# Chunk 0's copies shared by two engines, and ScalarE passes moved ahead of the first join

## The chip, the cores and the metric

The kernel runs on one core of a Trainium2 chip. The metric is the time of one execution on the device in microseconds; of several runs the median is taken. The core's engines are called TensorE (PE, its weight loads PEld), VectorE (DVE), ScalarE (ACT), GpSimd (POOL) and SyncE (SP), as in the profile. Each takes its own instructions strictly in the order in which the program issues them; where one needs what another makes, it waits for it. SP issues most of the DMAs of this kernel, in order too.

## The reference

Two blocks, one behind the other: a linear attention with a delta rule (4 batches, 8 heads, 768 steps, head width 48), and a SwiGLU feed-forward block (3072 tokens, 384 in, 1536 within).

```python
def _attn_ref(q, k, v, beta):
    k_n = k / (np.linalg.norm(k, axis=-1, keepdims=True) + 1e-06)
    state = np.zeros((B, H, D, D), dtype=np.float32)
    for t in range(S):
        kt, vt, bt = (k_n[:, :, t], v[:, :, t], beta[:, :, t, None])
        y[:, :, t] = np.einsum('bhd,bhde->bhe', q[:, :, t], state)
        v_old = np.einsum('bhde,bhd->bhe', state, kt)
        state = state + bt[:, :, :, None] * np.einsum('bhd,bhe->bhde', kt, vt - v_old)

def _moe_ref(x, w_gate, w_val, w_out):
    g = x @ w_gate
    silu = g * (1.0 / (1.0 + np.exp(-g)))
    return (silu * (x @ w_val) @ w_out).astype(np.float32)
```

## The kernel before

**Tiling.** The 768 steps are cut into 12 chunks of 64. Within a chunk the recursion is turned into matrix products: a triangular 64 by 64 matrix per head and batch, made of products of k with itself, must be inverted; with the inverse Z, a chunk is a short row of products. The inverses are made for two chunks at once (a group g). `substitute` (L483) does the forward substitution of blocks of 32 by 32 on DVE, in 31 steps of two operations (L488, L494); a join then makes the lower left block of each 64 by 64 inverse on PE.

**One chunk.** `advance(c)` (L708) is a generator; each `step("advance", advance, c)` runs it to its next yield. Its parts: for c over 0 the products with the old state; then p_u, the inverse times v (L741), copied to uu (L752), and the loads of v of chunk c+2 (`load_v`, L160); then p_y (L760), copied to y with its halves turned (L793, L795); then six transposes p_f (L805), copied to xts[c], shown as x_ffn (L808), which is the input of the feed-forward block for this chunk's 256 tokens. For chunk 0 a fifth part makes the first state (`of_state`, L769, copied by ACT at L783). The name `each` (L750) splits the copies of chunk 0 by bp, the pair of batches.

**Feed-forward.** `gate_val(c, f, fill, within)` (L818) makes p_gate and p_val in 12 matmuls each (L825), sil on ACT (L834) and h on DVE (L840). Between its parts it calls `fill` and `point`, which put other work at these places of each engine's order. `output` (L848) makes the result.

**Weights.** The three weight matrices are brought in as pieces: 0 to 11 are 256 columns wide (w_gate and w_val in turn), 12 to 23 are 512, and from 24 on pieces of w_out. A piece is loaded as 32-bit words into whatever tile is free (`stage`, L222; `place_of` names the place, `freed_by` the piece behind which a place is free again) and then converted. `power_step(n)` (L236) is the part on ACT: two passes, one that writes into the weight tile (L244) and one that writes an array of powers into one of the tiles hp[10] to hp[13] (L250). `convert(ns)` (L252) calls it for its pieces if it has not been done, does three operations for each piece on DVE (L261, L269, L281), calls `power_step` for some pieces ahead (L277 to L279), and then stages the pieces whose places have come free. Pieces 0 to 11 use hp[10] to hp[13] in turn, two to a tile; pieces 12 and 13 use hp[10] and hp[12].

**The order around the change.** Nothing is scheduled by a planner here: the block under `tc.manual_schedule` (L1112) is the order of every engine. After the substitution of group 0 (with ACT's passes of pieces 0 to 3 put into its middle, L1170), it runs: `turned_m(1, "ffn")` (L558), PE transposes that leave the matrix M of group 1 in two banks of PSUM, to be copied to mb; the scaling of v (L374); `turned(1, True, "px")`, q of chunk 1, copied by ACT at L412. Then `late_z` (L572): two DVE transposes, into zt (L574) and d_t (L580). Then `join_late(0, 0, ...)` (L583) for chunk 0, in two parts. Its first part copies half of d_t to d_o (L591, two copies), makes a first product (L598), and scales it into t2 (L600, shown as t). Its second part makes p_j (L608) and copies it into the upper right block of zt (L616, four copies: e, the parity of the head, by two quarters of the partitions). The generator `first_q` holds chunk 0's product of q and k: its second part is the masking on DVE (L437) into p_sb, which p_y reads.

The rest of the order before the first gate is six calls `converts(2)` with the steps of `advance` for chunk 0 and the copies of M between them, at L1182 to L1199. `invert(1)` (L619) begins with POOL's square root n_b of M's diagonal (L633); the rest of it comes much later, through `fill`. `second` is the join of chunk 1; it is run through the list `first`, inside the first `gate_val`, together with chunk 0's state.

The lines of the order that matter:

```python
        for _ in late_z(0, zb):
            pass
        mb = new_mb()
        mbs.append(mb)
        first_join = join_late(0, 0, ("px", "py"))
        next(first_join)
        converts(2)
        next(first_q)
        next(first_join)
        nc.scalar.copy(mb[:, m_1[0][0]], m_1[0][1])
        step("advance", advance, 0)
        converts(2)
```

Of the kernel before, what the change touches and what calls it, by code (L numbers as in the profile page):

```python
# [20 lines left out]
def kernel(  # L21
# [25 lines left out]
    nc = tc.nc  # L47
# [130 lines left out]
    pieces = []  # L178
# [4 lines left out]
    N_HALF = sum(piece[4] < PIECE for piece in pieces)  # L183
# [65 lines left out]
        )  # L249
        nc.scalar.activation(power, words_of[:, :, 0], ACTF.Copy, scale=2.0**-29)  # L250

    def convert(ns):  # L252

        work_of = []
        for n in ns:
            dst, _, t, f0, m = pieces[n]
            power_step(n)
            place = staged.pop(n)[:, 0:m]
            work_of.append((dst[:, t, f0 : f0 + m].bitcast(U32), place, powers.pop(n)))
        for dst, place, _ in work_of:  # L260
            nc.vector.tensor_scalar(  # L261
                out=place,
                in0=dst,
                scalar1=3,
                scalar2=None,
                op0=ALU.logical_shift_left,
            )
        for dst, place, _ in work_of:
            nc.vector.scalar_tensor_tensor(  # L269
                out=dst,  # L270
                in0=dst,
                scalar=0x80000000,
                in1=place,
                op0=ALU.bitwise_and,
                op1=ALU.bitwise_or,
            )
        for n in range(ns[-1] + 1, ns[-1] + 7):  # L277
            if n < min(N_HALF, len(pieces)) or ns[-1] + 3 > n < len(pieces):
                power_step(n)  # L279
        for dst, _, power in work_of:  # L280
            nc.vector.tensor_tensor(out=dst, in0=dst, in1=power, op=ALU.add)  # L281
        for n in ns:
            for later in freed_by.get(n, ()):
                stage(later)
# [27 lines left out]
    def half_of(x):  # L312
        return slice(64 * x, 64 * x + 64)
# [74 lines left out]
    def turned(c, of_q, tag=None):  # L388

        tag = tag or ("py" if of_q else "px")  # L390
        x = qpad[c % QB] if of_q else knp[slot(c)]
        if of_q:
            xt = work.tile([128, NB * NJ * 2 * C], FP32, name="qt", bufs=1)
        else:
            xt = kts[slot(c)]
        if c >= blocks_of[of_q][1]:
            xt_v = xt.rearrange("p (bp b j i) -> p bp j b i", bp=NB, b=2, j=NJ)
            (qt if of_q else kt)[c] = xt_v
            blocks = blocks_of[of_q][2]
            nc.vector.transpose(xt, blocks.rearrange("p bp h d -> p (bp h d)"))  # L400
            if c + 1 < NCH:
                load_blocks(of_q, c + 1)
            return
        xt = xt.rearrange("p (bp j b i) -> p bp j b i", bp=NB, j=NJ, b=2)
        (qt if of_q else kt)[c] = xt
        p_t = banks("p_t", tag)
        for bp in range(NB):
            for j in range(NJ):
                at = slice(128 * j, 128 * j + 128)
                nc.tensor.transpose(p_t[bp][:, at], x[:, bp, 2 * j : 2 * j + 2], ident)  # L410
        for bp in range(NB):
            nc.scalar.copy(xt[:, bp].rearrange("p j b i -> p (j b i)"), p_t[bp])  # L412
        if of_q and c + QB < Q_BLOCKS:
            load_q(c + QB)
# [46 lines left out]
    z1s, mbs = {}, []  # L461
    WAIT = 2

    def new_mb():
        return work.tile([128, R, R], FP32, name="mb", bufs=1)
# [114 lines left out]
        nc.vector.transpose(z_late[g], zb)  # L580
        yield

    def join_late(g, c, tags):  # L583


        zt, a, d_t = ztp[g % ZB], a_sb[g], z_late[g]
        M = HH // 2
        d_o = work.tile([128, M, R], FP32, name="d_o", tag="z1", bufs=1)
        d_v = d_t[:, :, HH * c : HH * c + HH].rearrange("p k (m e) -> p e m k", e=2)
        for s in range(2):  # L590
            nc.scalar.copy(d_o[QUADS[2 * s + 1][0]], d_v[QUADS[2 * s][0], 1])  # L591
        p_j = banks("p_j", tags[0])[0][:, 0 : M * R].rearrange("p (m i) -> p m i", i=R)
        for m in range(M):
            for e in range(2):
                for s in range(2):
                    dst, lo = QUADS[2 * s + e][0], QUADS[2 * s + 1][0]
                    h = 2 * m + e
                    nc.tensor.matmul(p_j[dst, m], a[lo, c, h, 0:R], zt[lo, c, h, R:C])  # L598
        t2 = work.tile([128, M, R], FP32, name="t2", tag="tmp", bufs=1)
        nc.scalar.mul(t2, p_j, -1.0)  # L600
        yield
        p_j = ps_pair("p_j", tags[1]).rearrange("p e (m i) -> p e m i", i=C)
        for of_d in (True, False):
            for m in range(M):
                for e in range(2):
                    for s in range(2):
                        row, hi = QUADS[2 * s + e][0], QUADS[2 * s][0]
                        nc.tensor.matmul(  # L608
                            p_j[hi, e, m, 0:R] if of_d else p_j[hi, e, m, R:C],
                            d_o[row, m] if e else d_t[row, :, HH * c + 2 * m],  # L610
                            ident[row, row] if of_d else t2[row, m],
                        )
        zt_v = zt[:, c].rearrange("p (m e) i -> p e m i", e=2)
        for e in range(2):
            for hi in (QUADS[0][0], QUADS[2][0]):
                nc.scalar.copy(zt_v[hi, e], p_j[hi, e])  # L616
        yield

    def invert(g):  # L619
# [88 lines left out]
    def advance(c):  # L708
# [80 lines left out]
            of_state()  # L789
        p_of_u()  # L790
        y = work.tile([128, NB, NJ, 2, D], FP32, name="y", tag="r", bufs=2)
        for bp in each:
            nc.scalar.copy(y[:, bp, :, 0], p_y[:, 0, bp])  # L793
            for b in range(2):
                nc.scalar.copy(y[half_of(b), bp, :, 1], p_y[half_of(1 - b), 1, bp])  # L795
        yield

        y_f = y.rearrange("p bp j par d -> p bp (j par d)")
# [5 lines left out]
                at = slice(t * 128, (t + 1) * 128)  # L804
                nc.tensor.transpose(p_f[:, t, bp], y_f[:, bp, at], ident)  # L805
        x_v = xts[c].rearrange("p t (bp n) -> p t bp n", bp=NB)
        for bp in each:
            nc.scalar.copy(x_v[:, :, bp], p_f[:, :, bp])  # L808
        yield
        if c == 0:  # L810
            of_state()
# [172 lines left out]

    todo = list(range(len(pieces)))

    def converts(n):
        if todo:
            convert(todo[:n])
            del todo[:n]  # L990

    gens = {}
# [119 lines left out]
    with tc.manual_schedule(  # L1112
# [60 lines left out]
        m_1 = turned_m(1, "ffn")  # L1173
        scale_v_heads(0)
        turned(1, True, "px")
        for _ in late_z(0, zb):
            pass
        mb = new_mb()
        mbs.append(mb)
        first_join = join_late(0, 0, ("px", "py"))  # L1180
        next(first_join)
        converts(2)  # L1182
        next(first_q)
        next(first_join)
        nc.scalar.copy(mb[:, m_1[0][0]], m_1[0][1])
        step("advance", advance, 0)
        converts(2)
        step("advance", advance, 0)
        nc.scalar.copy(mb[:, m_1[1][0]], m_1[1][1])
        converts(2)  # L1190
        step("advance", advance, 0)
        converts(2)
        step("advance", advance, 0)
        converts(2)
        second_inverse.append(invert(1))
        for _ in range(2):
            next(second_inverse[0])
        second = join_late(0, 1, ("ffn", "py"))
        converts(2)  # L1199

        def state_and_join():
# [73 lines left out]
```

## Time and profile before

| | |
|---|---|
| median of 3 runs | 737.07 us (736.52 to 737.8) |
| the profiled execution | 735.33 us, its span 733.5 us |
| mean granted clock of PE | 0.97 |
| PE busy | 696.3 us (95% of the span) |
| PEld busy | 603.8 us (82%) |
| DVE busy | 447.2 us (61%) |
| ACT busy | 167.4 us (23%) |
| POOL busy | 54.2 us (7%) |
| moved by DMA | 37.19 MB, mean 51 GB/s |

The span is the time from the first to the last instruction in the trace, and 1.8 us less than the execution's own time. A wait is written as engine, tile and line, an arrow, and what released it. A group of instructions is written as line, engine, operation, out <- in with partitions and elements, and how often. The share of busy time is an average over stages with very different limits; the stages to look at here lie between 40 and 80 us.

### The profile page before, as it was taken

The page shows a single profiled execution, that of the slowest core. Times are in us where ns is not written, and L with a number is a line of the kernel's source. Part 1 is how long each engine was busy: PE and PEld are TensorE (multiplying, and loading weights), DVE is VectorE, ACT ScalarE, POOL GpSimd, SP SyncE. Part 2 cuts the span into 40 slices and gives each one's busy share as a digit, 9 for nine tenths or more (in the row PEclk, how much of TensorE's full clock was granted, in tenths as well). Part 3 has the DMA queues.
Part 4 walks back from the last instruction along what each step waited for, and adds up shares of the span by engine and source line. Part 5 has one row for each costly group of instructions (what it writes and reads, how often), then busy time and mean ns, then how long its engine had stood idle before and what let it go on. Part 6 is the DMA issues. An engine that isn't in the chain of part 4 may idle for free.

```text
span 733.5 us, 22491 instructions
## 1 busy us (share of the span) xinstructions
PE 696.3 (95%) x10132; PEld 603.8 (82%) x10132; DVE 447.2 (61%) x904; ACT 167.4 (23%) x323; POOL 54.2 (7%) x46
## 2 busy tenths in 40 slices
PE   4757999999999999999999999999999999999997
PEld 3646888856787789988989988988988988989987
DVE  5995756797597252769853678853678853313122
ACT  3567664202401102021012021012021012021010
POOL 7003000203000000040000040000040000000000
PEclk9557999999999999999999999999999999999999
DMA  6786453310231112421202331202211100100000
GB/s 147 174 242 174 98 142 109 40 26 19 51 46 24 23 23 45 61 51 25 42 4 45 49 64 20 46 3 45 44 25 19 26 3 3 23 2 0 23 1 21
DMA packets 130736, 37.19 MB, mean 51 GB/s; under 512 B 122864, under 2 KB 125936, under 8 KB 130640
## 3 DMA queue, kind: packets, MB, share of 16 engines
q1 hardware_dynamic: 127184, 34.01, 22.7%
q10 hardware_dynamic: 3072, 1.57, 1.0%
q8 instruction: 79, 1.29, 0.8%
q0 software_dynamic: 384, 0.17, 0.1%
q14 instruction: 17, 0.14, 0.1%
HBM read 31.01 MB, written 4.72 MB: 49 GB/s over the span
## 4 chain that ended last, share of the span: by engine, by line
PE 84%; DVE 9%; ACT 4%; issue 2%; POOL 1%; DMA 1%; ACTq 0%; SPq 0%; DVEq 0%
PE p_gate L825 24%; PE p_val L825 23%; PE p_o L937 17%; PE p_o L854 6%; PE p_g L422 3%; DVE tmp L488 3%; DVE zb L494 3%; PE p_u L741 2%; PE p_r L720 2%; PE p_s L772 1%; PE p_y L760 1%; PE p_y L729 1%; POOL n_t L343 1%; PE p_f L805 1%; ACT last_h L250 1%
## 5 line engine op out<-in xcount | busy, mean ns | idle before, releaser
L825 PE MATMUL p_gate<-x_ffn,wg_sb 128*128 128x256 f32 x864 | 204.5, 387 | 1.3 <-ACT x_ffn L808 1.3
L825 PE MATMUL p_val<-x_ffn,wv_sb 128*128 128x256 f32 x864 | 198.5, 379 | 0.0
L825 PEld LDWEIGHTS p_val<-x_ffn,wv_sb 128*128 128x128 f32 x864 | 163.8, 190 | 22.3
L825 PEld LDWEIGHTS p_gate<-x_ffn,wg_sb 128*128 128x128 f32 x864 | 161.2, 191 | 24.1 <-ACT x_ffn L808 1.8
L840 DVE TENSOR_TENSOR h_f<-sil,p_val 128x512 f32<-128x512 f32 x71 | 48.5, 684 | 162.9 <-PE p_val L825 162.7
L834 ACT ACTIVATE sil<-p_gate 128x512 f32<-128x512 f32 x72 | 43.0, 597 | 292.2 <-PE p_gate L825 268.5
L937 PE MATMUL p_o<-wo_sb,h_f 128*128 128x192 f32 x432 | 75.6, 328 | 0.1
L937 PEld LDWEIGHTS p_o<-wo_sb,h_f 128*128 128x128 f32 x432 | 70.3, 190 | 1.2 <-DVE o_sb L947 0.7
L488 DVE TENSOR_TENSOR tmp<-zb,mb 128x31 f32<-128x31 f32 (+15 forms) x186 | 63.2, 340 | 12.0 <-PE p_j L608 6.7
L494 DVE TENSOR_TENSOR zb<-zb,tmp 128x31 f32<-128x31 f32 (+15 forms) x186 | 63.7, 342 | 6.4
L633 POOL TENSOR_TENSOR n_b<-mb,half 128x32 f32<-128x32 f32 x5 | 30.5, 6091 | 408.2 <-DVE mb L458 369.7
L947 DVE TENSOR_TENSOR o_sb<-o_sb,p_o 128x192 f32<-128x192 f32 x45 | 15.7, 349 | 53.7 <-PE p_o L937 36.5
L854 PE MATMUL p_o<-wo_sb,h_f 128*128 128x384 f32 x136 | 45.7, 490 | 0.0
L854 PEld LDWEIGHTS p_o<-wo_sb,h_f 128*128 128x128 f32 x136 | 25.3, 190 | 16.5
L937 PE MATMUL p_o<-last_k,h_f 128*128 128x192 f32 x180 | 32.2, 326 | 0.0
L937 PEld LDWEIGHTS p_o<-last_k,h_f 128*128 128x128 f32 x180 | 29.7, 190 | 0.0
L895 DVE TENSOR_TENSOR h_f<-h_f,h_f 128x256 f32<-128x256 f32 x54 | 22.4, 423 | 8.0 <-PE p_o L937 7.1
L937 PE MATMUL p_o<-last_h,h_f 128*128 128x192 f32 x144 | 26.3, 326 | 0.0
L937 PEld LDWEIGHTS p_o<-last_h,h_f 128*128 128x128 f32 x144 | 23.9, 190 | 0.0
L741 PEld LDWEIGHTS p_u<-vin,zt 64*64 64x64 f32 x768 | 13.7, 141 | 5.8 <-issue 3.2
L458 DVE STREAM_TRANSPOSE mb<-a_sb 32x1024 f32<-32x1024 f32 x8 | 17.1, 2139 | 0.2
L741 PE MATMUL p_u<-vin,zt 64*64 64x48 f32 x768 | 15.7, 228 | 1.3 <-ACT zt L616 1.1
(180 smaller groups left out, 673.4 us busy)
## 6 DMA issues: line engine op xcount, KB each, us to landing
vin<-in_v_dram SPq DMA_DIRECT2D x96, 48.0 KB
kn<-in_k_dram SPq DMA_DIRECT2D x40, 96.0 KB
out_dram<-o_sb SPq DMA_DIRECT2D x36, 96.0 KB
zt<-in_moe_w_out_dram SPq DMA_DIRECT2D x6, 384.0 KB
staged<-in_moe_w_out_dram SPq DMA_DIRECT2D x6, 384.0 KB
qpad<-in_q_dram SPq DMA_DIRECT2D x36, 64.0 KB
wo_sb<-in_moe_w_gate_dram SPq DMA_DIRECT2D x4, 512.0 KB
wo_sb<-in_moe_w_val_dram SPq DMA_DIRECT2D x4, 512.0 KB
```

The costliest lines, as they stand in the source:

```text
L422: nc.tensor.matmul(p_v[par][half_of(b if of_q else b ^ par), bp, j], kt[c][half_of(par), bp, j, b], xt[half_of(par), bp, j, b],)
L458: nc.vector.transpose(out(rows, 0), in_(rows, 0))
L488: nc.vector.tensor_tensor(out=t_v, in0=zb[:, 0 : j + 1, j : j + 1].to_broadcast([128, j + 1, m]), in1=mb[:, j : j + 1, j + 1 : R].to_broad ...
L494: nc.vector.tensor_tensor(out=zb[:, 0 : j + 1, j + 1 : R], in0=zb[:, 0 : j + 1, j + 1 : R], in1=t_v, op=ALU.add,)
L633: nc.gpsimd.tensor_tensor(out=n, in0=mb.rearrange("p j i -> p (j i)")[:, 0 : R * R : R + 1], in1=half, op=ALU.pow,)
L741: nc.tensor.matmul(p_u[half_of(b), par, bp, j], zt[half_of(b ^ par), par, bp, j], r[half_of(b ^ par), par, bp, j], start=first, stop=True, ...
L825: nc.tensor.matmul(ps[name][:, i], w_sb[:, t, (f + i) * 128 : (f + i + 1) * 128], xts[c][:, t], start=(t == 0), stop=(t == KT - 1),)
L834: nc.scalar.activation(sil, ps[name], ACTF.Silu)
L840: nc.vector.tensor_tensor(out=hs[c, f], in0=sil, in1=ps["p_val"], op=ALU.mult)
L854: nc.tensor.matmul(p_o, hs[c, f - f % 2][:, f % 2, bp * 128 : (bp + 1) * 128], wo_sb[:, f], start=(f == 0), stop=(f == FT - 1),)
L895: nc.vector.tensor_tensor(out=out, in0=a, in1=b, op=ALU.subtract)
L937: nc.tensor.matmul(p[x, part], a(f - f % 2)[:, f % 2], b(f), start=not begun and f == 0, stop=f == FH - 1, skip_group_check=True,)
```

## The change

It has four parts, all of them in the stretch before the second gate.

- `power_step` for pieces 4 to 7 and the two copies of M into mb, on ACT, are issued ahead of `late_z`; before, they were issued behind the first part of the join and between the steps of chunk 0.
- In the join of chunk 0, one of the two d_o copies and two of the four zt copies (those with e = 1) go to DVE. The other joins keep ACT for all.
- In `advance` for chunk 0, y is copied by one ACT copy over both bp and two DVE copies of the turned halves, and x by one copy on each engine. For the other chunks the instructions stay.
- The order: `first_q`'s masking now comes behind the second part of the join; the six conversions are moved back by about one step of chunk 0, so that those of pieces 6 to 11 come after x; and the first three conversions no longer start the passes of later pieces (`ahead=False`).

```diff
-    def convert(ns):
+    def convert(ns, ahead=True):
...
         for n in range(ns[-1] + 1, ns[-1] + 7):
-            if n < min(N_HALF, len(pieces)) or ns[-1] + 3 > n < len(pieces):
+            near = n < min(N_HALF, len(pieces)) or ns[-1] + 3 > n < len(pieces)
+            if ahead and near:
                 power_step(n)
...
-    def join_late(g, c, tags):
+    def join_late(g, c, tags, other=nc.scalar.copy):
...
-        for s in range(2):
-            nc.scalar.copy(d_o[QUADS[2 * s + 1][0]], d_v[QUADS[2 * s][0], 1])
+        for s, copy in enumerate((nc.scalar.copy, other)):
+            copy(d_o[QUADS[2 * s + 1][0]], d_v[QUADS[2 * s][0], 1])
...
-        for e in range(2):
+        for e, copy in enumerate((nc.scalar.copy, other)):
             for hi in (QUADS[0][0], QUADS[2][0]):
-                nc.scalar.copy(zt_v[hi, e], p_j[hi, e])
+                copy(zt_v[hi, e], p_j[hi, e])
...
-        for bp in each:
-            nc.scalar.copy(y[:, bp, :, 0], p_y[:, 0, bp])
-            for b in range(2):
-                nc.scalar.copy(y[half_of(b), bp, :, 1], p_y[half_of(1 - b), 1, bp])
+        nc.scalar.copy(y[:, :, :, 0], p_y[:, 0])
+        turn_half = nc.vector.tensor_copy if c == 0 else nc.scalar.copy
+        for b in range(2):
+            turn_half(y[half_of(b), :, :, 1], p_y[half_of(1 - b), 1])
...
-        for bp in each:
-            nc.scalar.copy(x_v[:, :, bp], p_f[:, :, bp])
+        if c == 0:
+            nc.scalar.copy(x_v[:, :, 0], p_f[:, :, 0])
+            nc.vector.tensor_copy(x_v[:, :, 1], p_f[:, :, 1])
+        else:
+            nc.scalar.copy(x_v, p_f)
...
-    def converts(n):
+    def converts(n, ahead=True):
         if todo:
-            convert(todo[:n])
+            convert(todo[:n], ahead)
...
         turned(1, True, "px")
+        for i in range(4, 8):
+            power_step(i)
+        mb = new_mb()
+        mbs.append(mb)
+        for part, p_m in m_1:
+            nc.scalar.copy(mb[:, part], p_m)
         for _ in late_z(0, zb):
             pass
-        mb = new_mb()
-        mbs.append(mb)
-        first_join = join_late(0, 0, ("px", "py"))
+        first_join = join_late(0, 0, ("px", "py"), copy_v)
         next(first_join)
-        converts(2)
+        converts(2, False)
+        next(first_join)
         next(first_q)
-        next(first_join)
-        nc.scalar.copy(mb[:, m_1[0][0]], m_1[0][1])
         step("advance", advance, 0)
-        converts(2)
         step("advance", advance, 0)
-        nc.scalar.copy(mb[:, m_1[1][0]], m_1[1][1])
-        converts(2)
+        converts(2, False)
         step("advance", advance, 0)
-        converts(2)
+        converts(2, False)
         step("advance", advance, 0)
         converts(2)
         second_inverse.append(invert(1))
         for _ in range(2):
             next(second_inverse[0])
         second = join_late(0, 1, ("ffn", "py"))
+        converts(2)
         converts(2)
```

## The prediction

> **What bounds the kernel now.** I read the page first: PE is busy 95% of the span and carries 84% of the chain that ended last, so nothing on another engine counts unless PE waits for it. Where PE waits is a matter of stages: in its 40 slices PE falls below nine tenths only in the first few. So I cut the stages around the change, from the chain of waits, and asked for busy times and granted clock in each. Columns: stage, its length, then busy time and count of PE, PEld, DVE, ACT and POOL, clock, DMA share, GB/s.
>
> ```profile
> 42.30:46.24 3.94, 1.00 (x64) 0.97 (x64) 3.80 (x7) 0.00 (x1) 0.00 (x0) 0.50 1.12 346
> 46.24:61.84 15.60, 9.40 (x269) 7.64 (x263) 11.89 (x38) 13.74 (x36) 5.62 (x1) 0.50 0.50 100
> 61.84:74.32 12.48, 11.42 (x281) 9.42 (x281) 8.41 (x16) 9.97 (x18) 0.01 (x1) 0.86 0.84 235
> ```
>
> The stage 46.24 to 61.84 runs from the end of the inverse to the first gate matmul. PE works 9.40 of 15.60 us there, at half clock; ACT is busy 13.74. Just before it ACT does nothing for 3.94 us. After it PE works 11.42 of 12.48 us. Then the waits of PE between 40 and 80 us (total, times, longest):
>
> ```profile
> PE p_f L805 <- ACT y L795: 2.1, 1, 2.1
> PE p_j L608 <- ACT d_o L591: 1.7, 4, 0.6
> PE p_u L741 <- ACT zt L616: 1.1, 2, 0.9
> PE p_gate L825 <- ACT x_ffn L808: 0.9, 1, 0.9
> PE p_y L760 <- ACT uu L752: 0.6, 1, 0.6
> ```
>
> All are ACT's copies of chunk 0. Now ACT itself in order of time:
>
> ```profile
> 41.21 1.07 ACT L412 COPY qt<-p_t 128x512 f32<-128x512 f32 x2 [1.80 <-PE p_t L410]
> 46.24 1.29 ACT L591 COPY d_o<-d_t 32x256 f32<-32x256 f32 x2 [3.96 <-DVE d_t L580]
> 47.55 0.38 ACT L600 ACTIVATE t<-p_j 128x256 f32<-128x256 f32 x1
> ...
> 50.60 2.36 ACT L616 COPY zt<-p_j 32x512 f32<-32x512 f32 x4
> ...
> 54.79 0.86 ACT L752 COPY uu<-p_u 128x384 f32<-128x384 f32 x2
> ...
> 60.93 0.86 ACT L808 COPY x_ffn<-p_f 128x384 f32<-128x384 f32 x2 [1.63 <-PE p_f L805]
> ...
> 66.43 0.60 ACT L834 ACTIVATE sil<-p_gate 128x512 f32<-128x512 f32 x1 [2.43 <-PE p_gate L825]
> ...
> 71.14 1.29 ACT L591 COPY d_o<-d_t 32x256 f32<-32x256 f32 x2
> ```
>
> ACT has two idle gaps: 3.96 us before the first d_o copy, and 2.43 us before sil. In between it has no gap but the short ones while PE makes y's and x's input. Later, beyond 80 us, PE's list of waits adds up to about 4 us in all and none of it is for a DMA, so a shift of the second gate (74.32) should reach the end whole. Last, what DVE pays for copies out of PSUM (busy, mean ns of one):
>
> ```profile
> L445 DVE COPY a_sb<-p_g 128x512 f32<-128x512 f32 x12 | 7.7, 683 | 2.3 <-PE p_g L422 2.3
> L702 DVE COPY zt<-p_j 32x1024 f32<-32x1024 f32 x4 | 4.9, 1222 | 4.5 <-ACT zt L702 4.5
> ```
>
> **What the Trainium skill says.** "PSUM — Partial Sum Buffer", the section on the PSUM accumulator: ScalarE and VectorE can read PSUM side by side at full rate if they are in different banks. The change splits zt by e, y by par and x by bp, and each index is one bank of its pair, so the copies may overlap; no run shows it yet. "VectorE: DVE Perf Modes", "Why PSUM operands drop a tier": an fp32 read of PSUM gets no faster mode. The two rows above agree: 512 more elements cost 539 ns. "TensorE: Matmul & The Clock Gate", Part 1: the array runs at half clock until about 3.4 us of sustained work, in windows that start freely. The trace agrees: 0.50 in every stage until about 65 us, 1.00 from 66 us, after a gate that starts at 61.84.
>
> **The change part by part.** Times are those of the profiled execution.
>
> *Passes of pieces 4 to 7 and both mb copies move ahead of late_z.* They were behind the first join: eight passes from 47.96 to 50.60, two mb copies at 52.98 and 55.53. Now they fall in ACT's first gap. It opens when the qt copies end, 42.28; eight passes take 2.63 (33.05 to 35.68 for the same eight of pieces 0 to 3), two 128x512 copies 1.07 (L412's pair): end 45.92. d_t is ready at 46.20, so they are hidden with 0.28 us to spare; any lateness above that is paid in full. No DMA is issued by them. mb must be free, which it is when substitute's last reading of it ends at 42.9. POOL's n_b (5.63 us at 56.22) starts near 46; its reader is at 135.44, and POOL has nothing else queued.
>
> *d_o.* Two ACT copies in a row (1.29) become one on ACT, one on DVE right behind d_t. DVE's price for a strided 32x256 is not shown: between 0.28 (L261, 256 unstrided) and ACT's 0.63; either end is hidden beside ACT. PE goes on at 46.93 and not 47.58: 0.65. Its two products took from 47.58 to 50.32, with 0.57 of issue in the middle. I let that gap move along (the other end: it stays in place, and up to 0.57 is lost). End 49.67.
>
> *zt.* ACT was late by 0.3 because of the passes, then took 2.36 for four copies. Now ACT has two (1.15) and DVE two: 683 each, back to back about 1.30 (the two mask products L437 take 1.28). DVE is free: conversion 0,1 (1.72) ends near 48.4. 49.72 to 51.02, against 52.96. What waits behind these copies on DVE is the p_sb mask: 51.02 to 52.30; p_y needs it at 53.05, so 0.75 spare.
>
> *p_u, uu, p_y.* Before, 52 of 64 p_u were left after the last zt copy (1.73); now some 60 at 30 ns: 51.07 to 53.05. The first uu copy no longer stands behind passes, so p_y starts at once and not 0.58 later; 1.96 as before: end 55.05, against 57.28.
>
> *y.* Six ACT copies, 57.35 to 59.30, become one of 128x384 on ACT (0.48) and two of 64x384 on DVE: 0.683 less 128 elements at 1.05 ns, 0.55 each, 1.05 together: 55.10 to 56.15. DVE is idle then: masks, then conversion 2,3 until 54.1.
>
> *p_f and x.* p_f 1.54: 56.20 to 57.74. DVE meanwhile converts 4,5, six operations in 1.74: 56.15 to 57.90. So DVE's half of x starts 0.15 late and takes 0.55: 58.45. **First gate 58.50 against 61.84: 3.34 earlier.**
>
> *What is pushed back.* Conversions 6 to 11 and the passes of 8 to 11, done beside the chain before, now follow x. On ACT: eight passes from 58.2 to 60.85; the first pass of 12 to 61.4; its second writes the buffer of 8 and 9, so it waits for DVE's conversion 8,9 (two conversions of 1.74 after 58.45: 61.95); then three passes to 63.70. Behind this stand sil, six passes, state and the second d_o, and PE stops at the second join for d_o, as it did (1.07 of the 1.7 above). The gate ends at 58.50 + 4.5 = 63.0; sil starts at 63.65 against 66.43, so this end gains 2.78 and not 3.34. Everything up to the second gate follows sil on ACT without a gap: 71.54 against 74.32. DVE keeps pace: 10,11 until 63.7, 12,13 until 66.8, 14 until 68.3, h to 68.9, 15,16 to 72.0 (before 74.67).
>
> *DMAs.* SP's order stays: piece 22, v of chunk 2, 23, 17. v is asked for 1.7 us earlier. Piece 17 waits for conversion 11 and leaves at 63.7 and not 61.26; its first pass is near 70.1. 256 KB at the 235 GB/s of that stage is about 1.1 us: covered. Piece 18 leaves at 65, as before, and is read near 71.2.
>
> *Chunks after 0.* y keeps three ACT copies and x one: nothing changes.
>
> Sum: 2.8 us off 735.33 (span 733.5) is 732.5. The median, 737.07, is 1.74 above the profiled execution; taken off there: **734.3**.
>
> **Rivals.**
> 1. *PE's clock rises earlier.* p_u and p_y now run 4 us without a gap, just above the page's 3.4. For it: the length; against it: the window starts freely, and DVE's conversion 4,5 then bounds x. At most p_y halves: 0.9 more, 733.4.
> 2. *The backlog on ACT eats it.* If the 2.64 us of passes behind x find no cover (the gap before sil was 2.43 and would have to be lost to waits for DVE), 3.34 - 2.64 = 0.7 is left: 736.4. Against it: DVE's queue has no long wait there.
> 3. *The sharing doesn't share:* DVE's copies stand behind conversions, or two engines on one PSUM pair slow each other. Then only ACT's passes out of the way count: 0.3 before zt, 0.4 at uu, 0.3 of d_o: about 1.0, 736.1. Against it: the DVE ends above, each at most 0.15 after its input.
> 4. *Slower: the moved block makes the first join late.* It starts behind qt, which waits for PE's p_t, which waited 2.4 us for the load of q 1 while the DMA share was 0.98. ACT had 3.96 us of slack; now 0.28. If the load lands x later than here, x - 0.28 is paid. It turns slower beyond x = 3.1; with x = 4, 0.9 us: 738.0. Against it: x must then be more than the whole wait of 2.4; the three runs say nothing here, since the old slack hides such a lateness.
>
> **Numbers.** Forecast 0.70; clock 0.10; backlog 0.08; no sharing 0.05; slower 0.07. A measurement here can tell about 0.2% (1.5 us) from no change. Faster: the first two, 0.80; same: the next two, 0.13; slower 0.07. Bounds around the forecast: the issue gap staying (0.57 less), the slack of 0.28 missed by half a us, a later clock rise, which lengthens the gate but is hidden behind ACT by up to 0.6 (0.6 more), DVE copies 0.1 off each. That gives 733.0 to 735.6; with the clock's case and the backlog's, 732.6 to 736.4.
>
> **What would show it.** Right: PE's wait for y falls from 2.1 to about 1.1 us, that for uu goes, that for the first d_o falls from 0.7 to about 0.4; first gate near 58.5; the gap before sil gone; PE still waits about 1 us at the second d_o, second gate near 71.5, and the same distance from there to the end. Wrong: the first d_o starts later than 46.5; ACT's four passes of 12 and 13 end after 64.5; the distance from second gate to end grows.

## The result, and the profile after

No change that can be told from none: the changed kernel took 737.06 us (median of 6 runs, 736.19 to 739.08), the kernel before, run beside it, 736.74 us (735.87 to 737.8). The ratio is 1.0009, with a 95% interval of 0.9993 to 1.0025. The profiled execution of the changed kernel took 736.72 us, with a span of 734.8 us.

The line numbers have moved: d_o is copied at L592, zt at L617, y at L793 (ACT) and L796 (DVE), x at L809 (ACT) and L810 (DVE); the gate is L829. First the stages, cut at the same events as before the change: end of the qt copies, first d_o, first gate, second gate. Columns as in the prediction: length, busy times and counts of PE, PEld, DVE, ACT and POOL, clock, DMA share, GB/s.

```profile
43.18:46.80 3.62, 1.32 (x68) 1.17 (x68) 3.56 (x4) 3.59 (x12) 0.00 (x0) 0.50 1.14 312
46.80:62.66 15.86, 8.74 (x259) 7.35 (x259) 9.69 (x26) 4.63 (x11) 5.56 (x1) 0.50 0.48 98
62.66:76.03 13.37, 12.25 (x280) 9.84 (x280) 13.30 (x34) 12.17 (x24) 0.00 (x0) 0.81 0.64 204
```

ACT's 3.94 us of idleness are filled (3.59 busy). Its work in the stage of chunk 0 has fallen from 13.74 to 4.63 us. And yet that stage is no shorter: 15.86 us against 15.60. PE is busy in 8.74 us of it, so 7 us are still waits. These are PE's waits between 40 and 80 us that bear on it (total, times, longest; 1.1 us of the first line lie at the second join, behind 72 us):

```profile
PE p_j L609 <- ACT d_o L592: 2.0, 3, 0.9
PE p_f L806 <- DVE y L796: 1.8, 1, 1.8
PE p_j L609 <- issue: 1.5, 1, 1.5
PE p_gate L829 <- DVE x_ffn L810: 1.2, 1, 1.2
PE p_u L742 <- ACT zt L617: 0.7, 1, 0.7
PE p_y L761 <- ACT uu L753: 0.6, 1, 0.6
PE p_u L742 <- DVE zt L617: 0.5, 2, 0.3
```

The same five waits are there as before; two have another engine's name, and none is gone. The wait for y was to fall from 2.1 to 1.1 us and is 1.8, the one for uu was to vanish and is 0.6, the one for x has grown from 0.9 to 1.2. Now the two engines that share the copies, in order of time, ACT first. The bracket is the idle time before, and what ended it.

```profile
42.11 1.07 ACT L413 COPY qt<-p_t 128x512 f32<-128x512 f32 x2 [2.94 <-PE p_t L411]
...
45.70 1.07 ACT L1185 COPY mb<-p_m 128x512 f32<-128x512 f32 x2
46.80 0.63 ACT L592 COPY d_o<-d_t 32x256 f32<-32x256 f32 x1
...
51.20 1.18 ACT L617 COPY zt<-p_j 32x512 f32<-32x512 f32 x2 [3.36 <-PE p_j L609]
...
58.20 0.48 ACT L793 COPY y<-p_y 128x384 f32<-128x384 f32 x1 [1.70 <-PE p_y L761]
61.53 0.48 ACT L809 COPY x_ffn<-p_f 128x384 f32<-128x384 f32 x1 [2.85 <-PE p_f L806]
...
66.18 0.68 ACT L250 ACTIVATE h_f<-wo_sb 128x512 uint32<-128x512 uint32 x1 [1.00 <-DVE wv_sb L282]
```

```profile
46.22 0.37 DVE L592 COPY d_o<-d_t 32x256 f32<-32x256 f32 x1
...
52.41 1.40 DVE L617 COPY zt<-p_j 32x512 f32<-32x512 f32 x2 [3.88 <-ACT zt L617]
...
58.71 1.12 DVE L796 COPY y<-p_y 64x384 f32<-64x384 f32 x2 [1.84 <-ACT y L793]
...
62.04 0.56 DVE L810 COPY x_ffn<-p_f 128x384 f32<-128x384 f32 x1 [0.34 <-ACT x_ffn L809]
```

Two things stand here. The three copies out of PSUM do not run side by side: each time DVE starts when ACT has ended (51.20 and 52.41, 58.20 and 58.71, 61.53 and 62.04), and in each bracket what ended DVE's idleness is ACT's copy of the same tile. Only d_o, which lies in SBUF, is copied by both independently: DVE begins right behind d_t, at 46.22, and in e3_shares (below) ACT starts at 46.24 and DVE at 46.25. And ACT's d_o begins at 46.80, 0.6 us after d_t was ready: the qt copies ended at 43.18 here and at 42.28 before, and the moved block stands behind them without a gap. The chain of waits (start, length, what) shows the two together:

```profile
46.80 0.64 ACT d_o L592
...
47.48 0.69 PE p_j L609 x33
48.17 1.47 issue
49.64 1.53 PE p_j L609 x85
...
51.20 0.57 ACT zt L617
...
51.80 0.59 ACT zt L617
...
52.41 0.68 DVE zt L617
...
53.12 0.70 DVE zt L617
```

The four zt copies follow one another as they did when ACT made all of them, and within p_j PE has a gap of issue of 1.47 us (0.57 before) for which the profile names no releaser.

Behind 80 us nothing has moved: PE's waits there add up to 3.7 us (before 4.1), and from the second gate to the end of the span it is 658.8 us (before 659.2).

### The profile page after: what moved, and what is told of

Its sections match the earlier page's. It is cut to its first block, busy times and chain, and to the rows that moved or that the text cites. A ratio compares the mean times of both kernels' runs of the same rounds, so it can differ in the third digit from the quotient of the medians.

```text
span 734.8 us, 22483 instructions
## 1 busy us (share of the span) xinstructions
PE 698.0 (95%) x10132; PEld 605.2 (82%) x10132; DVE 450.7 (61%) x910; ACT 164.1 (22%) x314; POOL 54.2 (7%) x46
## 4 chain that ended last, share of the span: by engine, by line
PE 85%; DVE 7%; ACT 3%; issue 2%; SPq 2%; DMA 1%; ACTq 0%; DVEq 0%
PE p_gate L829 24%; PE p_val L829 23%; PE p_o L941 15%; PE p_o L858 6%; PE p_g L423 3%; PE p_u L742 2%; PE p_y L761 2%; DVE tmp L489 2%; PE p_r L721 2%; PE p_s L773 1%; PE p_y L730 1%; DVE zb L495 1%; SPq L119 1%; DVE h_f L899 1%; PE p_f L806 1%
## 5 line engine op out<-in xcount | busy, mean ns | idle before, releaser
L829 PE MATMUL p_gate<-x_ffn,wg_sb 128*128 128x256 f32 x864 | 205.4, 388 | 1.5 <-DVE x_ffn L810 1.2
L829 PE MATMUL p_val<-x_ffn,wv_sb 128*128 128x256 f32 x864 | 198.5, 379 | 0.0
L829 PEld LDWEIGHTS p_val<-x_ffn,wv_sb 128*128 128x128 f32 x864 | 163.8, 190 | 22.3
L829 PEld LDWEIGHTS p_gate<-x_ffn,wg_sb 128*128 128x128 f32 x864 | 161.6, 192 | 24.5 <-DVE x_ffn L810 1.6
L753 ACT COPY uu<-p_u 128x768 f32<-128x768 f32 (+1 forms) x13 | 9.6, 750 | 35.0 <-PE p_u L742 35.0
```

Of the source, the lines that this page charges most:

```text
L829: nc.tensor.matmul(ps[name][:, i], w_sb[:, t, (f + i) * 128 : (f + i + 1) * 128], xts[c][:, t], start=(t == 0), stop=(t == KT - 1),)
```

## The experiments

Fourteen profiles of kernels like these (both above among them) put the end of the qt copies anywhere from 42.2 to 47.1 us. It is not a load that moves it: in all of them PE's transposes of q of chunk 1 start right behind p_m, without a wait, and the qt copies end 2.9 to 3.1 us after that start. What differs are gaps of issue, of 0.6 to 3.0 us in p_g and 1.9 to 4.4 us in p_m. Before the change (PE's order):

```profile
38.77 0.46 PE L566 MATMUL p_m<-ident,a_sb 32*32 32x32 f32 x17 [1.92 <-issue]
39.15 1.97 PE L410 MATMUL p_t<-ident,qpad 128*128 128x128 f32 x8
```

So one profile beside another tells of lengths and orders, and the medians tell of times. "Before" is always the kernel before, run on the same chip beside it.

**One part alone.** Is it the sharing or the moved block that fails? e2_moves keeps the moves and gives all copies to ACT as before; e3_shares keeps ACT's old order and shares the copies; e4_before is the kernel before once more.

```diff
 e2_moves, against the changed kernel
-        nc.scalar.copy(y[:, :, :, 0], p_y[:, 0])
-        turn_half = nc.vector.tensor_copy if c == 0 else nc.scalar.copy
-        for b in range(2):
-            turn_half(y[half_of(b), :, :, 1], p_y[half_of(1 - b), 1])
+        for bp in each:
+            nc.scalar.copy(y[:, bp, :, 0], p_y[:, 0, bp])
+            for b in range(2):
+                nc.scalar.copy(y[half_of(b), bp, :, 1], p_y[half_of(1 - b), 1, bp])
...
-        first_join = join_late(0, 0, ("px", "py"), copy_v)
+        first_join = join_late(0, 0, ("px", "py"))
 e3_shares, against the kernel before (inside join_late, and for y and x, as in the change)
-        first_join = join_late(0, 0, ("px", "py"))
+        first_join = join_late(0, 0, ("px", "py"), copy_v)
```

> The changed kernel with all copies of chunk 0 back on ScalarE, in the form of before: the moves alone. Theory 1 (the sharing is worth nothing): within 0.5 us of the changed kernel; zt 2.4 us, y 2.0, x 0.9, d_o 1.3. Theory 2 (the sharing brings its 2.8 us, which chance hides): about 2.8 us slower than the changed kernel. Theory 3 (the moved block makes the first join late): the first d_o copy starts later than 46.24 us whenever the qt copies end after 42.5 us, by the same amount.

> The kernel before with the shared copies alone; the order of before stays, with the passes and the copies of M where they were. Theory 1: VectorE waits for ScalarE at zt, y and x, and also stands behind its conversions, so the time is that of before or up to 1 us more. Theory 2: about 2 us faster than before. Theory 3 (the moved block costs): the first d_o copy starts at 46.2 us here, right behind d_t.

> The kernel before once more, unchanged, for a second trace: how far the end of the qt copies, PE's gap of issue inside p_j, the length of the first gate and the start of the second gate move from one execution to the next. Theory 1 takes these as chance of about 1 us each way; theory 2 needs them to be near the values of the first trace (42.28, 0.57 us, 4.56 us, 74.32) and far from those of the changed kernel (43.18, 1.47 us, 5.41 us, 76.03).

| kernel | us | before | ratio, 95% |
|---|---|---|---|
| e2_moves | 736.99 | 736.67 | 1.0012 [1.0004, 1.0020] |
| e3_shares | 736.54 | 736.67 | 1.0000 [0.9992, 1.0008] |
| e4_before | 736.40 | 736.67 | 1.0000 [0.9992, 1.0009] |

The sharing alone is worth nothing that shows (its interval is 0.6 us to either side), and the moves alone cost 0.9 us by the ratio, in which the moved block and the backlog behind x are not told apart. In e3_shares' order of DVE the copies again begin when ACT's have ended, although ACT's order is the old one:

```profile
51.88 1.40 DVE L617 COPY zt<-p_j 32x512 f32<-32x512 f32 x2 [2.20 <-ACT zt L617]
...
58.18 1.12 DVE L796 COPY y<-p_y 64x384 f32<-64x384 f32 x2 [1.30 <-ACT y L793]
```

In e2_moves the qt copies ended at 44.83, and the moved block pushed d_o out to 48.42 (ACT's order):

```profile
43.76 1.07 ACT L413 COPY qt<-p_t 128x512 f32<-128x512 f32 x2 [4.82 <-PE p_t L411]
...
48.42 1.28 ACT L592 COPY d_o<-d_t 32x256 f32<-32x256 f32 x2
```

Set beside it e4_before, where the block is not in the way: qt ended at 43.83 there, later than the 43.18 of the changed kernel, and d_o began at 46.38, right behind d_t.

**Does the pair of banks make the copies take turns?** p_j, p_y and p_f are each one PSUM tile of two banks; the shared copies read one bank each. e1_banks gives chunk 0 two tiles of one bank each in their place. Every instruction of the changed kernel stays.

```diff
-        p_j = ps_pair("p_j", tags[1]).rearrange("p e (m i) -> p e m i", i=C)
+        p_j = [p.rearrange("p (m i) -> p m i", i=C) for p in banks("p_j", tags[1])]
...
-                copy(zt_v[hi, e], p_j[hi, e])
+                copy(zt_v[hi, e], p_j[e][hi])
...
-        p_y = recur(ps_pair("p_y", "py"))
+        p_y = recur_banks(banks("p_y", "ffn") if c == 0 else banks("p_y", "py"))
...
-            nc.scalar.copy(x_v[:, :, 0], p_f[:, :, 0])
-            nc.vector.tensor_copy(x_v[:, :, 1], p_f[:, :, 1])
+            nc.scalar.copy(x_v[:, :, 0], p_f[0])
+            nc.vector.tensor_copy(x_v[:, :, 1], p_f[1])
```

> The changed kernel, but chunk 0's p_j of the join, p_y and p_f lie each in two PSUM tiles of one bank in place of one tile of two banks; every instruction stays. Theory 1 (VectorE's copies wait for ScalarE's because both read the same PSUM pair, and the program makes such readers take turns): VectorE's zt copies start with ScalarE's and not after them; from the end of p_j to the last zt copy about 1.3 us and not 2.6, y about 1.1 and not 1.65, x about 0.6 and not 1.1; the first gate about 2.2 us earlier at an equal start of the join, the kernel 1.3 to 2.2 us faster than the changed one. Theory 2 (the copies share already, and a late instruction fetch and clock of the profiled runs hid a gain): the same three stretches stay at 2.6, 1.65 and 1.1 us, and the time stays at that of the changed kernel.

735.97 us against 736.67, ratio 0.9994 [0.9985, 1.0003]: by the two ratios 0.15%, or 1.1 us, better than the changed kernel, though their intervals overlap and 1.3 to 2.2 us were expected. From the first d_o to the first gate it is 14.5 us in place of 15.9, 1.3 us less where 2.2 were expected. What it did in the trace is plain. ACT's lines, then DVE's:

```profile
51.66 1.18 ACT L623 COPY zt<-p_j 32x512 f32<-32x512 f32 x2 [3.33 <-PE p_j L615]
...
58.17 0.48 ACT L799 COPY y<-p_y 128x384 f32<-128x384 f32 x1 [1.76 <-PE p_y L767]
60.39 0.48 ACT L819 COPY x_ffn<-p_f 128x384 f32<-128x384 f32 x1 [1.75 <-PE p_f L816]
```

```profile
51.72 1.40 DVE L623 COPY zt<-p_j 32x512 f32<-32x512 f32 x2 [2.61 <-PE p_j L615]
...
58.21 1.12 DVE L802 COPY y<-p_y 64x384 f32<-64x384 f32 x2 [2.03 <-PE p_y L767]
...
61.12 0.55 DVE L820 COPY x_ffn<-p_f 128x384 f32<-128x384 f32 x1
```

DVE now starts within 0.06 us of ACT, released by PE and not by ACT. zt takes 1.46 us (51.66 to 53.12) in place of 2.61, y 1.16 (58.17 to 59.33) in place of 1.63. Each copy lasts as long as before, so the two readers do not slow each other: that agrees with the Trainium skill, "PSUM — Partial Sum Buffer", which says at the end of "Specifications (TRN2)" (and not, as the prediction has it, in the section on the accumulator) that the two engines read PSUM in parallel at full rate as long as they do not meet in a bank. The bank isn't what made them take turns, since each copy read a bank of its own before as well; the tile is: where two copies read one tile, DVE's waits for ACT's. x is late for another reason here: with y earlier DVE has begun its next conversions, which end at 61.1, 0.7 us after ACT's half could start.

**Does the gap within p_j come from the loads?** Around 46 us SP issues the loads of v of chunk 1 and q of chunk 2. e6_bdma (from the kernel before) and e7_adma (from the changed one) put them behind the first conversion.

```diff
-        if of_q and c + QB < Q_BLOCKS:
+        if of_q and 0 < c and c + QB < Q_BLOCKS:
...
-        load_v(1)
...
+        load_v(1)
+        load_q(2)
```

> The kernel before, with one thing moved: the loads of v of chunk 1 and q of chunk 2 (12 DMAs) are issued behind the first conversion and not between 38 and 51 us. Theory 5 (PE's gap of issue inside p_j, 0.6 to 1.5 us, is its instructions waiting behind these loads): the gap goes or falls below 0.3 us, p_j ends at 49.6 us or a little later, the first gate 0.6 to 1.3 us earlier than in the two traces of before, the kernel up to 1.3 us faster. If the gap has another cause, it stays, and so does the time.

> The changed kernel with the same loads moved. Theory 5: the gap of 1.5 us in p_j goes, and now the earlier d_o counts: p_j ends near 49 to 49.7 us in place of 51.2, the kernel 1 to 2 us faster than the changed one. The waits of VectorE for ScalarE at zt, y and x stay: 2.6, 1.65, 1.1 us.

e6_bdma: 736.37 against 736.62, 0.9996 [0.9988, 1.0004], with a gap of 0.57 as before. e7_adma: 737.62, 1.0013 [1.0006, 1.0019]; in its profile there is no gap, but the qt copies ended at 46.08 and d_o began at 49.67, so PE's wait for d_o takes the gap's place:

```profile
PE p_j L609 <- ACT d_o L592: 4.8, 3, 3.1
```

Over all fourteen profiles the gap lies between 0.5 and 1.5 us, or there is none; none in the four in which the last d_o copy ended at 48.69 us or later. So p_j ends near the same time for an early d_o and a late one: in e3_shares d_o ended at 46.87 and zt began at 50.67, in e2_moves 49.70 and 51.77. 2.8 us of lateness came through as 1.1. Where the gap comes from is not settled; two kernels with the loads moved away (e10 and e11 below) had it at 1.50 and 1.44.

**Towards a better order.** All three of these start from e1_banks. e5_gaps puts the mb copies behind t2, ACT's passes 8 to 11 into its waits for p_u and p_y, and the conversion of pieces 4 and 5 ahead of y, so that less stands between x and sil. e8_all adds the moved loads to it, and puts the mask and the join's second part ahead of the first conversion. e9_late4 is e5_gaps with two things swapped: only the mb copies (1.1 us) stay ahead of late_z, and passes 4 to 7 go behind t2.

```diff
 e5_gaps, against e1_banks
-        mb = new_mb()
-        mbs.append(mb)
-        for part, p_m in m_1:
-            nc.scalar.copy(mb[:, part], p_m)
...
         next(first_join)
+        mb = new_mb()
+        mbs.append(mb)
+        for part, p_m in m_1:
+            nc.scalar.copy(mb[:, part], p_m)
...
+        power_step(8)
+        power_step(9)
         step("advance", advance, 0)
         step("advance", advance, 0)
         converts(2, False)
-        step("advance", advance, 0)
         converts(2, False)
+        power_step(10)
+        power_step(11)
+        step("advance", advance, 0)
         step("advance", advance, 0)
 e8_all, against e5_gaps
-        converts(2, False)
-        next(first_join)
         next(first_q)
+        next(first_join)
+        converts(2, False)
+        load_v(1)
+        load_q(2)
 e9_late4, against e5_gaps
-        for i in range(4, 8):
-            power_step(i)
-        for _ in late_z(0, zb):
-            pass
-        first_join = join_late(0, 0, ("px", "ffn"), copy_v)
-        next(first_join)
         mb = new_mb()
...
+        for _ in late_z(0, zb):
+            pass
+        first_join = join_late(0, 0, ("px", "ffn"), copy_v)
+        next(first_join)
+        for i in range(4, 8):
+            power_step(i)
```

> The changed kernel with the split PSUM tiles of e1_banks, and besides: the copies of M behind t2 in place of ahead of late_z, the passes of pieces 8 to 11 in ScalarE's waits for p_u and p_y in place of behind x, and the conversion of pieces 4 and 5 ahead of y in place of behind it. Theory 3 (the moved block makes the join late and this costs): d_o starts 0.5 to 1 us earlier than in e1_banks at an equal end of the qt copies, and p_j ends that much earlier. Theory 5 (p_j's end is set by the arrival of PE's instructions): d_o starts earlier, but the gap of issue in p_j grows by as much and p_j ends where it did. Theory 4 (the backlog on ScalarE costs at the second gate): from the start of the first gate to that of the second 12.9 us or less at a first gate of 4.8, in place of 13.06. VectorE's half of x no longer starts 0.7 us late. In all 0.5 to 1.5 us faster than e1_banks.

> e5_gaps with the same loads moved, and the masking ahead of the join's second part, the first conversion behind it. If the causes add up (split tiles 1.1 us as measured, gaps about 1, loads 1 to 1.5): p_j ends near 49.2, the first gate near 58 to 59 us, the kernel 2.5 to 4 us faster than before. If only one of them can show at a time, about 1 to 1.5 us faster than before.

> The changed kernel with split PSUM tiles as in e1_banks, and ScalarE's moved work cut in two: only the two copies of M (1.07 us) stay ahead of d_o, the passes of pieces 4 to 7 come behind t2; the passes of 8 to 11 and the conversion of 4 and 5 in the gaps as in e5_gaps. Theory 3 (the moved block of 3.6 us makes the first d_o late whenever the qt copies end after 42.5 us): d_o starts right behind d_t, near 46.2, even if the qt copies end at 44 to 45; the kernel is 0.3 to 1 us faster than e1_banks. Theory 5 (p_j ends when PE's instructions have come): d_o early, but p_j still ends between 50.3 and 51.3 us, and the gain over e1_banks is only that of the gaps behind it, about 0.5 us.

e5_gaps: 736.08 against 736.62, 0.9999 [0.9986, 1.0011]: a miss. Its p_j lies in the banks that p_m had, and now waits until mb has been copied out of them; e8_all's first uu copy stands behind passes 8 and 9, which wait for a conversion. The two lines, e5_gaps and then e8_all:

```profile
PE p_j L615 <- ACT mb L1199: 1.7, 2, 1.5
```

```profile
PE p_y L767 <- ACT uu L759: 1.5, 1, 1.5
```

e8_all is nevertheless faster than before, 735.24 us and 0.9983 [0.9975, 0.9991]: about 1.3 us, what was expected if only one of the causes shows. So is e9_late4, 735.97 against 736.76 and 0.9987 [0.9981, 0.9994]; its profile doesn't show the early d_o that it was made for, since its qt copies ended at 47.06 us and ACT's d_o began at 48.07.

e10_late4_loads is e9_late4 with the loads moved as in e7_adma. e11_d_o is e10 with the second join's d_o copied by DVE already ahead of the first zt copies, into a buffer of its own:

```diff
+        d_o_1 = late_d_o(0, 1, (copy_v, copy_v), "d_o_1")
         next(first_join)
...
-        second = join_late(0, 1, ("ffn", "py"))
+        second = join_late(0, 1, ("ffn", "py"), d_o=d_o_1)
```

> e9_late4 with the loads of v of chunk 1 and q of chunk 2 moved behind the first conversion, as in e6_bdma. Theory 5: the gap of issue in p_j falls to the 0.57 us that is left where no load is in the way, p_j ends near 49.5 to 50, about 0.7 us faster than e9_late4, near 734.5 to 735. If the loads have no part in it: the time of e9_late4.

> e10_late4_loads, and d_o of the second join (chunk 1) copied by VectorE in its wait for the first p_j, and no longer by ScalarE behind the state. PE's waits for the second d_o (about 1.1 us in every trace so far) go; what is late next is t2 behind the state copy. From first to second gate about 1 us shorter at an equal first gate; the kernel 0.5 to 1.1 us faster than e10_late4_loads.

e10: 734.16 us against 736.76, 0.9970 [0.9963, 0.9977]. e11: 733.94 against 736.76, 0.9965 [0.9951, 0.9978]; PE's waits for the second d_o are gone, what is late in their place is zt (first line: the wait between the second gate and the next product), and the second gate is 11.25 us behind the first (60.91) and not 13.1. The lines are from PE's waits and its order of time:

```profile
PE p_g L423 <- ACT zt L629: 1.0, 1, 1.0
```

```profile
72.16 2.86 PE L845 MATMUL p_gate<-x_ffn,wg_sb 128*128 128x256 f32 x12
```

By the medians that is worth no more than 0.2 us over e10, within the intervals, where 0.5 to 1.1 were expected. In e11's profile the span ends 661.3 us behind the second gate (659.2 before): nearly all of the 2.2 us won up to there is lost later, 1.7 us of it at one gate (last section); that execution took 735.38 us. e11 is the fastest of all: 2.6 us (0.35%) off the time before.

**e10 once more.** Its profiled execution, 736.72 us, was one of two above 735.4 in its 22, and its first gate, at 61.68 us, came hardly earlier than before. So the same kernel was profiled a second time.

> The kernel of e10 again, for a second profile: of e10's 22 executions the one profiled (736.7 us) and one more (737.5) lie 2 to 3 us above the other twenty (733.6 to 735.3), so its trace need not show what the median shows. Theory 5a: with the loads of v and q moved away, most executions have no gap of issue within p_j and an early p_m, and the profiled one was an exception. Then an execution near 734 shows the gap at 0 to 0.6 us instead of 1.5, the qt copies ended before 44.8 instead of 46.5, and the first gate near 60 instead of 61.7. Rival 5b: the gap of issue stays at about 1.5 us and the first gate stays near 61.7; the 2 us lie behind the second gate (where the profiled execution of e10 had a stall of PE at 12 matmuls that took 4.54 us), so the second gate starts at about 74.7 in both and its length falls to about 3 us. If the profile again falls on an execution above 736.5 us, it tells nothing of the two.

734.43 us against 736.68, ratio 0.9968 [0.9954, 0.9983]; the profiled execution took 734.93. ACT's order in it, and PE's wait and second gate:

```profile
41.42 1.07 ACT L413 COPY qt<-p_t 128x512 f32<-128x512 f32 x2 [2.34 <-PE p_t L411]
42.73 1.07 ACT L1192 COPY mb<-p_m 128x512 f32<-128x512 f32 x2 [0.23 <-DVE tmp L489]
46.03 0.62 ACT L598 COPY d_o<-d_t 32x256 f32<-32x256 f32 x1 [2.23 <-DVE d_t L587]
...
49.79 1.18 ACT L623 COPY zt<-p_j 32x512 f32<-32x512 f32 x2
```

```profile
PE p_j L615 <- issue: 0.9, 1, 0.9
```

```profile
59.87 4.32 PE L839 MATMUL p_gate<-x_ffn,wg_sb 128*128 128x256 f32 x12 [0.74 <-DVE x_ffn L820]
...
72.94 4.54 PE L839 MATMUL p_gate<-x_ffn,wg_sb 128*128 128x256 f32 x12
```

Theory 5a holds in the main: qt ends 4 us earlier than in e10's first profile, ACT waits 2.23 us for d_t behind the mb copies, so nothing stands in the join's way, and both gates come 1.8 us earlier (61.68 and 74.75 there). The gap is 0.9 us, neither of the two values expected. That the qt copies of this kernel end early more often than e9's, because of the moved loads, would fit the 1.8 us between their medians. But the profiles don't bear it out: with the loads moved the gap in p_m is 2.2 to 3.9 us in six, without 1.9 to 4.4 in eight; and e6_bdma and e7_adma gained nothing by the same move. Why e10 is faster than e9 stays open.

## Why the prediction was wrong

Forecast 734.3 us, measured 737.06, above even the widest bound that it gave, 736.4. The first gate was to start at 58.50 and started at 62.66. The 4.16 us between them, term by term along the prediction's own path:

| step | predicted | profile after | late by |
|---|---|---|---|
| first d_o on ACT (0.28 to spare) | 46.20 | 46.80 | 0.6 |
| gap of issue within p_j | 0.57 | 1.47 | 0.9 |
| zt, first copy to last | 1.30 | 2.61 | 1.3 |
| p_u, uu, up to p_y | 2.03 | 2.36 | 0.3 |
| y, first copy to p_f | 1.10 | 1.78 | 0.7 |
| x, first copy to gate | 0.76 | 1.13 | 0.4 |

The first two rows are in part chance, since they move from profile to profile. The three rows of shared copies make 2.4 us.

**The step that failed: "the copies may overlap".** zt, y and x were each reckoned as the longer of two halves beside each other. They are the sum of the two: 1.18 and 1.40 for zt. The durations were right (zt 683 ns a copy on DVE estimated, 0.68 and 0.70 measured; y 0.55, measured 0.56; d_o within its bounds, 0.37). And with copies in turn DVE's are dearer than ACT's: four on ACT took 2.36 us. The prediction had a rival near this, "two engines on one PSUM pair slow each other", at 0.05; the mechanism is another (they do not slow each other, one waits), and not even the 1.0 us that this rival left came. e1_banks shows the cause: the wait hangs on the shared tile. A row that the prediction quoted gave warning of it: the later joins' zt is shared already, and DVE's idle time there, 4.5 us before four copies, is put down to `ACT zt L702`. It was a warning and no proof, since each engine reads both banks there. The row was read for its price, 1222 ns, and its second half passed over.

**The same at uu.** p_y was to start "at once and not 0.58 later", since ACT's passes had gone. It waits 0.6 us as before, and so it does in e1_banks and e2_moves. The first uu copy starts when all of p_u has ended (p_u to 55.62, uu from 55.64), and p_y when that copy (0.49) has: the copy itself is what it waits for. It was so before the change as well: p_u ended at 54.74 and uu began at 54.79, so the passes ahead of uu had cost next to nothing, and the prediction misread the wait.

```profile
53.01 1.73 PE L741 MATMUL p_u<-vin,zt 64*64 64x48 f32 x52 [0.15 <-ACT zt L616]
```

That p_u's one tile keeps the copy from starting sooner is likely by the above, but was not tried.

**The moved block had no slack.** "0.28 us to spare; any lateness above that is paid in full" was right as a mechanism (rival 4): e2_moves shows it in its trace, and the moves alone cost 0.9 us. (By the prediction's own terms the block ends at 45.98 and not 45.92, so 0.22 us were to spare.) Wrong was where the slack was read. The first profile's end of the qt copies, 42.28, is all but the earliest of fourteen (42.2 to 47.1), and the block of 3.6 us stands behind it each time: 46.80, 47.29, 48.42, 49.67 in four kernels. Wrong too was the reason that rival 4 gave for a late qt, a wait of 2.4 us for the load of q: that wait is at 18 us, before the transposes of q of chunk 0. Those of chunk 1 waited for no load; they stand behind p_m and its gap of issue, so the 2.4 us set no bound on how late qt can be. "Paid in full" was too hard, on the other hand: the gap within p_j swallows a part.

**The earlier d_o gave little or nothing.** Its 0.65 us were booked with the gap moving along; the other end, "it stays in place", was named and priced at 0.57. It stayed in place, and more: zt began at 50.60 in the first profile and at 50.67 in e3_shares, whose last d_o copy ended 0.66 us earlier. (Against e4_before, where d_o ended at 47.67 and zt began at 51.08, it is 0.4 us won of 0.8.)

**What was right, and what was luck.** The backlog behind x seems to have cost nothing: from the first gate's start to the second's, less the first gate's own length, it is 7.97 us against 7.92 before, and 8.54 was predicted. That is luck. The first gate took 5.40 us and not 4.5, and so covered the passes: sil follows at 68.09, just as the gate ends. In e7_adma, with ACT's order of the changed kernel, the gate took 4.65 us and ended at 68.46; sil started 0.6 us later, the second gate at 77.00, and the distance is the predicted 8.54 us. The first line is from PE's order, the second from ACT's:

```profile
63.81 4.65 PE L829 MATMUL p_gate<-x_ffn,wg_sb 128*128 128x256 f32 x12 [1.16 <-DVE x_ffn L810]
```

```profile
69.07 0.59 ACT L838 ACTIVATE sil<-p_gate 128x512 f32<-128x512 f32 x1
```

So the backlog was priced rightly, and it is a cost of the change that one long gate hid. ACT's pass of 12 did wait for a conversion, 1.00 us where 0.55 was reckoned, and sil followed without the old gap. The moved DMAs did no harm, and the later chunks are as they were.

The length of the first gate is chance: its 12 matmuls took 4.3 to 5.5 us in the fourteen profiles, as the clock rises at another moment in each. Before the change the granted clock was 0.84 from 65 to 66 us, 3.2 to 4.2 us after the gate's start; after it, it was still 0.54 from 66 to 68 us, 3.3 to 5.3 us after the start. That is in line with the Trainium skill, "TensorE: Matmul & The Clock Gate", Part 1, whose windows start freely. (The prediction's "0.50 in every stage until about 65 us" holds for the stages that it cut, not for the first 20 us, where the trace has 0.94.)

The forecast of "slower" at 0.07 was not far wrong in its mechanism; 0.80 for "faster" rested on one untested claim three times over.

## What to carry to other kernels

Before a copy out of PSUM is shared between two engines, look for a tile in the profile that is shared already and read what ends the second engine's idleness; if it is the first engine, give each engine a tile of its own bank before anything else. A slack taken from one profile is one draw: the end of the qt copies moved over 4.9 us in fourteen profiles, and work placed behind such an event and ahead of a join must fit the late case. Where several gains rest on one unseen behaviour, their chances are one chance, not many.

## What the runs showed of the hardware

- **Two readers of PSUM.** ScalarE and VectorE copied from two banks side by side, each as fast as alone (zt 1.18 us for ACT's two copies and 1.40 for DVE's, in e1_banks as in the changed kernel); from one tile of two banks they took turns, 2.61 us in place of 1.46.
- **Gaps of issue in long runs of matmuls.** PE stopped for 0.5 to 1.5 us behind the 37th matmul of chunk 0's p_j in ten of fourteen profiles, and for 1.9 to 4.4 us ahead of the last 17 matmuls of p_m in all, with nothing that the profile names. The place is the same each time, so it goes with the place in PE's instructions and not with the data; that PE waits for the instructions themselves, as theory 5 of the expectations has it, was not shown. The one in p_m sets when q's transposes, and so the qt copies, are done; the DMA share around it is 0.8 to 1.05. The cause of neither was found.
- **A whole gate at half clock.** After the clock had risen, 12 gate matmuls took 4.54 us and not 2.86 in four profiles: at the second gate in both profiles of e10, behind waits for d_o of 1.35 and 1.48 us, and at 188 us in e9_late4 and e11_d_o, behind two waits of 0.5 us. The granted clock was 0.62 over that gate in e10's second profile. The waits alone do not decide it: in e7_adma a wait of 1.27 us at the second join, and in e3_shares and e8_all the same two waits of 0.5 us near 188 us, left the gate at 2.86 (the line is e7_adma's wait, in PE's order). What else it takes is not shown, nor whether this is what sets executions of one kernel 2 to 3 us apart.

```profile
74.50 0.24 PE L609 MATMUL p_j<-ident,d_o 32*32 32x32 f32 x2 [1.27 <-ACT d_o L592]
```
